# Opening of attention with other score banks, load order and transposes; next first operand ahead of the second matrix in units 1 to 4

## The chip, the cores and the metric

The kernel runs on one NeuronCore of one Trainium2 chip. The metric is the device time of one execution in microseconds (us). Engines are named as in the profile: PE (TensorE matmul), PEld (its weight loads), DVE (VectorE), ACT (ScalarE), POOL (GpSimd) and SP (SyncE, which only issues DMAs here). Each engine works through its own instructions in program order and waits on semaphores of the others.

## The reference, cut

Inputs: q, k, v of 4 batches, 8 heads, 576 positions, 64 wide; expert weights of 8 experts 512 to 1024 to 512; a last feed-forward of 512 to 2048 to 512 whose weights come as 64-bit floats.

```
scores = scale * q @ k.T                       # window of 128, causal, with a slope per head
attn   = softmax(where(mask, scores + bias, -1e9))
x      = (attn @ v) as 2304 tokens x 512
logits = x @ w_gate;  P = exp(logits - max);   8 rounds of row and column normalisation
x      = sum over 8 experts of P[:, e] * (relu(x @ w1[e]) @ w2[e])
h      = x @ w_in;  out = (h * cos(h)) @ w_out
```

## The kernel before

**Attention** (the first 156 us). Two heads make a pair; there are 16 pairs, and each has five groups of queries (u = 0 to 4), so 80 groups n. The loop takes two groups per turn i (n = 2i and 2i+1), and the program's order is that of the calls in it. A turn issues the scores of its groups on PE (`emit_qk`, L537 and L535), the exponentials of the turn before on ACT (`emit_exp`, L562), the maxima of its own groups on DVE (`emit_max`, L547), a step of the gate (`gates`), attention times v of turn i-4 (`emit_AV`, L639), the PE transposes of the next pair's q and k (`heads` and `emit_T`, L494; pieces 0 and 1 are q, 2 and 3 are k), the transposes of the probabilities of turn i-3 (`emit_PT`, L601 and L603), the normalisation on POOL (`emit_norm`, L586) and side work (`side`). A tile's name carries the pair or the group: T2_0 is piece 0 of pair 2, s6_0 a score bank of groups 6 and 7, pt0 the transposed probabilities of group 0.

**Banks.** PSUM has eight banks: two for scores (`ps_s`), three for transposes and probabilities (`ps_t`), two for `xbank` (where attention times v accumulates and pieces 1 and 3 of the transposes land), one for the gate and pieces 0 and 2 (`ps_g`). The scores of turns 1 and 3 are put into one half of `xbank` and one bank of `ps_t`, all others into `ps_s`. A piece in `xbank` waits for whoever still reads `xbank`.

**Loads.** All loads but the first k go through SP's queue, in program order. `load_heads` issues three DMAs for one operand of one pair into one of two buffers; q of pair p+2 is loaded behind the transposes of q of pair p+1. `load_raw` loads expert weights (two DMAs of 256 KB), `load_f64` a piece of the 64-bit weights into the buffer `u0`, and `convert_f64` turns one piece into 32-bit numbers in ten steps, one step per group, and loads the next piece in its eighth step.

**Gate.** `gates` first finishes an earlier half of 384 tokens (`gate_block2`: three small matmuls, a DVE copy L384) and then begins the next half (`gate_block`, L374), both in the one bank of `ps_g`.

**Experts.** The phase `moe, 0` has 32 units u; each takes seven products of 384 columns (L972, tiles x, y, z), and one `batch` of the unit before: six tiles of 128 tokens in `g2` (L1200 to L1202) into the banks gT0, gT1, gT2 in turn, each added to an accumulator by DVE (`evac`, L1181, later L1191). Beside it the next unit's operands are made in high and low halves: `prep_a` (first operand waX: three ACT copies L143, three DVE subtractions L146, a store L148), `prep_b` (second matrix wbX: ACT L160, POOL L162, three stores L167), `prep_s` and `prep_sb` (sums on POOL). They are generators in lists (`pre`, `sbq`), and `slot` takes a step of the first of each list between products and tiles. In `pre`, `prep_b` of a unit stands ahead of `prep_a` of the next. In units 0 to 3 eight rounds of `sinkhorn` (PE L420; DVE L410 to L412 and L421 to L423) run in the list `bg`.

Of the kernel before, what the change touches and what calls it, by code (L numbers as in the profile page):

```python
# [18 lines left out]
P = 128  # L19
# [10 lines left out]
def tile_attention_moe_cos_ffn(ctx, tc, q, k, v, w_gate, w1, w2, w_in, w_out, out):  # L30
# [42 lines left out]
    with tc.manual_schedule():  # L73
# [164 lines left out]
        f64_t = {}  # L238

        def load_f64(c):  # L240
            if c >= 4 * NU2:
                return
            s, x = divmod(c, 4)
            raw = u_pool.tile([P, 512, 2], I32, tag="u0", name=f"f64_{c}")
            if x < 2:
                for y in range(2):
                    kc = 2 * x + y
                    nc.sync.dma_start(
                        out=raw[:, y * FU:(y + 1) * FU, :].rearrange("p n t -> p (n t)"),
                        in_=w_in[kc * P:(kc + 1) * P, 2 * s * FU:2 * (s + 1) * FU],  # L250
                    )
            else:
                r0 = s * FU + (x - 2) * P
                nc.sync.dma_start(out=raw.rearrange("p n t -> p (n t)"), in_=w_out[r0:r0 + P, :])
            f64_t[c] = raw
# [266 lines left out]
        def emit_qk(n, pi, u):  # L522
            a = n % 2
            if n // 2 not in sbank:
                if n // 2 in (1, 3):
                    sbank[n // 2] = [xbank[:, :512], ps_t.tile([P, 512], F32, tag="t", name=f"s{n}_1")]
                else:
                    sbank[n // 2] = [ps_s.tile([P, 512], F32, tag="s", name=f"s{n}_{j}") for j in range(2)]
            grp[n] = sbank[n // 2] if a == 0 else sbank.pop(n // 2)
            c0, c1 = span(u)  # L530
            k0 = (u - 1) * P + c0
            for j in parts(u):
                o = grp[n][j][:, a * W2 + c0:a * W2 + c1]
                if u == NG - 1:
                    nc.tensor.matmul(o, qL[pi % 2], kT[pi][:, k0:k0 + c1 - c0])  # L535
                else:
                    nc.tensor.matmul(o, qT[pi % 2][hr[j], u * P:(u + 1) * P], kT[pi][hr[j], k0:k0 + c1 - c0])  # L537
# [126 lines left out]
        load_heads(0, k, kraw, "kr", nc.scalar, part=1)  # L664
        load_heads(1, q, qraw, "qr")
        load_heads(1, k, kraw, "kr")
        load_heads(0, v, vt, "v")
        make_identity(nc, ident)
        warm = ps_s.tile([P, 512], F32, tag="s", name="warm")

# [53 lines left out]
        distance(rel_li, rel_l, LW, hr)  # L724
        for t in qL:
            nc.gpsimd.memset(t, 0.0)
        load_heads(1, v, vt, "v")

        groups = [(pi, u) for pi in range(NP_ALL) for u in range(NG)]
        done_tok = 0  # L730
# [9 lines left out]
        def heads(n, pool=None):  # L740
            if n >= NGR:
                return
            pi, u = groups[n]
            if u < 4 and pi + 1 < NP_ALL:
                emit_T(pi + 1, u, pool)
                if u == 1:
                    load_heads(pi + 2, q, qraw, "qr")
                if u == 3:
                    load_heads(pi + 2, k, kraw, "kr")

        def side(n):
            nonlocal conv
            if n % 2 == 0 and n < 2 * NPAIR:
                set_last(n // 2)
            if n == 2:
                nc.sync.dma_start(out=wg_raw, in_=w_gate.rearrange("(k p) e -> p k e", p=P))
                nc.gpsimd.memset(wg, 0.0)
            if n == 3:
                load_f64(0)
            if 4 <= n < 8:  # L760
                load_raw((n - 4) // 2, "ab"[n % 2])
            if n == 8:
                nc.gpsimd.tensor_copy(wg[:, :, :E], wg_raw)
            if n == 12:
                conv += [prep_s(0), prep_a(0), prep_b(0), prep_s(1), prep_a(1), prep_b(1), prep_s(2)]
            if n == 48:
                early.append(stages(("moe", 0), xr[0]))
            if n == NGR:
                conv.append(prep_sb(0))
            if n == 56:  # L770
                early.append(combos(("moe", 0), xr[0]))
            if early and next(early[0], StopIteration) is StopIteration:
                early.pop(0)
            if 8 <= n < 50 and (chunk or n < 40):
                if not chunk:
                    chunk.append(convert_f64(n_f64[0]))
                    n_f64[0] += 1
                if next(chunk[0], StopIteration) is StopIteration:
                    chunk.pop(0)
            if n % 2 == 0 or 44 <= n < 56 or n >= 72:  # L780
                while conv and next(conv[0], StopIteration) is StopIteration:
                    conv.pop(0)

        def gates(n):
            nonlocal gate2, next_half
            for j, lT in gate2:
                gate_block2(j, lT, (ps_g, "g"))
            gate2 = []
            if n < NGR + 6 and next_half < 2 * NB and HB * (next_half + 1) <= done_tok:
                gate2.append((next_half, gate_block(next_half, (ps_g, "g"), ap_)))  # L790
                next_half += 1

# [3 lines left out]
        for i in range(NGR // 2 + 4):  # L796
            for g in pair(i):
                emit_qk(*g)
            for g in pair(i - 1):
                if g[0]:  # L800
                    emit_exp(*g)
            for g in pair(i):
                if g[0] != 1:
                    emit_max(*g)
            gates(2 * i - 2)
            if not i:
                emit_exp(*pair(0)[0])
                emit_T(0, 1, (ps_t, "t"))
                emit_T(0, 3, (ps_g, "g"))
                emit_max(*pair(0)[1])  # L810
            for g in pair(i - 4):
                emit_AV(*g)
            if i == 1:
                heads(0)
                heads(1)
                heads(2, (ps_t, "t"))
            elif i:
                if i == 2:
                    heads(3)
                heads(2 * i)  # L820
                heads(2 * i + 1)
            for n, pi, u in pair(i - 4):
                if u == NG - 1:
                    emit_x(pi)
                    load_heads(pi + 2, v, vt, "v")
                    if pi % NPAIR == NPAIR - 1:
                        done_tok += S
            for g in pair(i - 3):
                emit_PT(*g)
            if i < NGR // 2:  # L830
                emit_norm(pair(i - 1))
            else:
                for g in pair(i - 1):
                    emit_norm([g])
            for n in (2 * i, 2 * i + 1):
                side(n)
# [392 lines left out]
        def begin(n):  # L1229
            if n < len(steps):  # L1230
                kind, b, u = steps[n]
                if kind == "moe" and not b and u >= 2:
                    pre.append(prep_a(u))
            if n + 1 < len(steps):
                kind, b, u = steps[n + 1]
                if not b and kind == "moe" and u >= 3:
                    pre.append(prep_s(u))
# [168 lines left out]
```

## Time and profile before

| what | us |
|---|---|
| runs shown: median (lowest to highest of 3) | 1981.72 (1981.71 to 1982.1) |
| the profiled execution | 1982.96 |
| its span, first to last instruction | 1981.2 |
| attention, to the first expert product | 0 to 156.1 |
| expert phases and last feed-forward | 156.1 to 1981.2 |

The span is what all rows refer to; what lies around it is 1.76 us in the profiled execution. A row of a timeline gives start, duration, engine, line, operation, tiles and shape; in brackets stands the idle time of the engine just before it and what ended that. Matmul ends are modelled, so two neighbouring matmuls may overlap by a few tenths.

### The profile page before, as it was taken

Reading aid. Unit: us, or ns where it says so; the run is one execution under the profiler, and the core shown is the slowest. Engines: PE = TensorE matmul, PEld = TensorE weight load, DVE = VectorE, ACT = ScalarE, POOL = GpSimd, SP = SyncE. Lnnn points to the kernel's source line nnn. Section 1 sums busy time; section 2 is a strip of 40 time slices with the busy share of each in tenths; the row PEclk is TensorE's granted clock in tenths of the full one; section 3 lists DMA queues with packets and bytes.
Section 4 is the critical chain, followed back from the end, with each engine's and each line's share of the span. In section 5 each row is a group of like instructions: output and inputs, shape, how many; then the busy total and the mean of one; then the engine's idle time right before and its main releaser. Section 6 shows DMA issues by size and latency. Waiting matters only on the chain.

```text
span 1981.2 us, 31148 instructions
## 1 busy us (share of the span) xinstructions
PE 1957.6 (99%) x10977; PEld 1823.6 (92%) x10977; DVE 1555.7 (79%) x2655; ACT 862.6 (44%) x1617; POOL 964.7 (49%) x940
## 2 busy tenths in 40 slices
PE   8999999999999999999999999999999999999999
PEld 6668899999999999999999999999999999998898
DVE  7885777777777788988888877888877776757766
ACT  6885444444444333333333433333233354554543
POOL 5673566666666445454536622545454423333221
PEclk9999999999999999999999999999999999999999
DMA  7854888888888999998999888999998765554552
GB/s 194 221 141 146 294 294 312 302 310 311 295 309 302 321 333 314 339 336 320 340 326 326 277 285 280 328 337 334 330 306 297 242 223 195 197 218 175 207 192 96
DMA packets 293755, 540.05 MB, mean 273 GB/s; under 512 B 80256, under 2 KB 141792, under 8 KB 286432
## 3 DMA queue, kind: packets, MB, share of 16 engines
q1 hardware_dynamic: 292240, 537.74, 78.7%
q8 instruction: 87, 1.43, 0.3%
q14 instruction: 68, 0.56, 0.1%
q10 hardware_dynamic: 1360, 0.33, 0.1%
HBM read 384.32 MB, written 153.67 MB: 272 GB/s over the span
## 4 chain that ended last, share of the span: by engine, by line
PE 94%; DVE 2%; DMA 2%; ACT 1%; issue 1%; SPq 0%; POOL 0%; DVEq 0%; POOLq 0%; ACTq 0%
PE gT L1111 23%; PE y_moe L972 19%; PE z_moe L972 10%; PE gT L1201 7%; PE gT L1202 7%; PE gT L1200 7%; PE y_ffn L972 5%; PE x_moe L972 5%; PE z_ffn L972 2%; PE xbank L639 2%; DMA wbX<-wdp 1%; PE x_ffn L972 1%; PE s L537 1%; PE pt L603 1%; PE pt L601 1%
## 5 line engine op out<-in xcount | busy, mean ns | idle before, releaser
L1111 PE MATMUL gT<-hX,wbX 128*128 128x384 f32 x2688 | 538.7, 335 | 2.8 <-DMA wbX<-wdp 2.7
L1111 PEld LDWEIGHTS gT<-hX,wbX 128*128 128x128 f32 x2688 | 471.6, 188 | 5.5 <-DMA wbX<-wdp 2.1
L972 PE MATMUL y_moe<-xtT_moe,waX 128*128 128x384 f32 x1728 | 347.3, 335 | 0.0
L972 PEld LDWEIGHTS y_moe<-xtT_moe,waX 128*128 128x128 f32 x1728 | 304.4, 188 | 3.3 <-ACT s_moe L1001 0.6
L1123 DVE TENSOR_TENSOR acc_moe<-gT,acc_moe 128x384 f32<-128x384 f32 x432 | 237.7, 550 | 77.9 <-PE gT L1111 76.0
L1202 PE MATMUL gT<-wbX,hX 128*128 128x512 f32 x660 | 258.2, 391 | 0.0
L1201 PE MATMUL gT<-wbX,hX 128*128 128x512 f32 x660 | 258.1, 391 | 0.0
L1200 PE MATMUL gT<-wbX,hX 128*128 128x512 f32 x660 | 258.0, 391 | 0.0
L1001 ACT ACTIVATE s_moe<-y_moe 128x384 f32<-128x384 f32 x192 | 93.3, 486 | 350.5 <-PE y_moe L972 350.2
L1145 POOL TENSOR_TENSOR hodd<-hodd 128x384 f32<-128x384 f32 x128 | 156.0, 1238 | 139.2 <-DVE hX L1131 71.3
L1145 POOL TENSOR_TENSOR cX<-cX 128x384 f32<-128x384 f32 x128 | 145.7, 1158 | 157.3 <-DVE hX L1131 97.1
L961 POOL TENSOR_TENSOR hX<-cX,hX 128x768 fp32r<-128x768 f32 x44 | 83.5, 1913 | 249.3 <-ACT hX L958 208.6
L133 POOL TENSOR_TENSOR s<-ra 128x256 f32<-128x256 f32 x80 | 59.6, 745 | 236.5 <-DVE waX L146 164.0
L1191 DVE SCALAR_TENSOR_TENSOR acc_moe<-gT,prob,acc_moe 128x512 f32<-128x512 f32 x174 | 129.6, 747 | 37.5 <-PE gT L1202 35.7
L1202 PEld LDWEIGHTS gT<-wbX,hX 128*128 128x128 f32 x660 | 123.9, 188 | 25.9
L1200 PEld LDWEIGHTS gT<-wbX,hX 128*128 128x128 f32 x660 | 124.1, 188 | 25.5 <-DVE acc_moe L1191 0.7
L1201 PEld LDWEIGHTS gT<-wbX,hX 128*128 128x128 f32 x660 | 124.0, 188 | 24.3
L917 ACT ACTIVATE hX<-cX 128x768 fp32r<-128x768 f32 x64 | 43.9, 687 | 216.1 <-DVE cX L1004 216.1
L1131 DVE TENSOR_TENSOR hX<-cX,hX 128x768 fp32r<-128x768 f32 x112 | 131.4, 1173 | 1.6 <-ACT hX L1135 1.6
L1131 DVE TENSOR_TENSOR hX<-hodd,hX 128x768 fp32r<-128x768 f32 x112 | 127.4, 1137 | 0.9 <-ACT hX L1135 0.9
L972 PE MATMUL z_moe<-xtT_moe,waX 128*128 128x384 f32 x576 | 116.6, 336 | 2.6 <-DVE waX L146 2.6
L972 PE MATMUL z_moe<-xtB_moe,waX 128*128 128x384 f32 x576 | 116.1, 336 | 0.0
(211 smaller groups left out, 3768.3 us busy)
## 6 DMA issues: line engine op xcount, KB each, us to landing
waX<-wd SPq DMA_DIRECT2D x264, 512.0 KB, 5.5
wbX<-wdp SPq DMA_DIRECT2D x224, 512.0 KB, 6.6
wd<-waX SPq DMA_DIRECT2D x32, 1792.0 KB, 6.8
wdp<-sb SPq DMA_DIRECT2D x32, 1024.0 KB, 5.8
wdp<-wbX SPq DMA_DIRECT2D x96, 256.0 KB, 4.3
wbX<-wd SPq DMA_DIRECT2D x24, 1024.0 KB, 4.9
waX<-wd SPq DMA_DIRECT2D x88, 256.0 KB, 5.2
ra<-in_moe_w_dram SPq DMA_DIRECT2D x64, 256.0 KB, 7.3
```

The costliest lines, as they stand in the source:

```text
L133: nc.gpsimd.tensor_tensor(out=s4[:, o], in0=x, in1=y, op=op)
L961: eng.tensor_tensor(out=h[:, 1], in0=c, in1=h[:, 0].bitcast(F32), op=ALU.subtract)
L972: nc.tensor.matmul(ps[:, :HB], wa[:, WI[m], wl, kc, :], x[:, xl, kc, :], start=start and kc == 0 and n_ == 0, stop=stop and kc == 1 and n_ ...
L1001: nc.scalar.activation(out=t["s", i], in_=ps[:, :HB], func=AF.Copy)
L1111: nc.tensor.matmul(ps[:, :HB], w[:, u, wl, d * P:(d + 1) * P], x[:, xl, u, :], start=m in (1, 5, 2) and n_ == 0, stop=m in (4, 3, 2) and n ...
L1123: nc.vector.tensor_tensor(out=a, in0=ps[:, :HB], in1=a, op=ALU.add)
L1131: nc.vector.tensor_tensor(out=x[:, 1], in0=H[:, q], in1=x[:, 0].bitcast(F32), op=ALU.subtract)
L1145: nc.gpsimd.tensor_tensor(out=H[:, t[0], c], in0=H[:, t[1], c], in1=H[:, t[2], c], op=ALU.subtract)
L1191: nc.vector.scalar_tensor_tensor(out=a, in0=ps, scalar=pe, in1=a, op0=ALU.mult, op1=ALU.add)
L1200: nc.tensor.matmul(ps, hf[f][:, 0, ts], wb[:, f, 0, :], start=f == 0, stop=False)
L1201: nc.tensor.matmul(ps, hf[f][:, 0, ts], wb[:, f, 1, :], start=False, stop=False)
L1202: nc.tensor.matmul(ps, hf[f][:, 1, ts], wb[:, f, 0, :], start=False, stop=f == 1)
```

## The change

In attention: the scores of turn 1 go into two banks of `ps_t`, those of turn 3 into `ps_s`; in turn 3 the probabilities' transposes stand ahead of the heads' transposes; q and k are loaded one pair earlier (pair p+3 into the buffer that pair p+1 has just left); v of pairs 0 and 1 goes behind q of pair 2; the first three 64-bit pieces are loaded into the token buffer `xr[NB - 1]`, which is free until the last batches, at fixed groups (0, 12, 22, 32) and no longer behind a conversion; expert weights are loaded at groups 4, 18, 28, 38, not 4 to 7; conversions begin one group later; `gates` finishes a half or begins one, not both in a call. In the expert phase `prep_a` of units 2 to 5 is put at the head of `pre`.

```diff
         def load_f64(c):
-            if c >= 4 * NU2:
+            if c >= 4 * NU2 or c in f64_t:
                 return
             s, x = divmod(c, 4)
-            raw = u_pool.tile([P, 512, 2], I32, tag="u0", name=f"f64_{c}")
+            if c < 3:
+                spare = xr[NB - 1].rearrange("p k t -> p (k t)")[:, c * 1024:(c + 1) * 1024]
+                raw = spare.bitcast(I32).rearrange("p (n t) -> p n t", t=2)
+            else:
+                raw = u_pool.tile([P, 512, 2], I32, tag="u0", name=f"f64_{c}")
...
             if n // 2 not in sbank:
-                if n // 2 in (1, 3):
-                    sbank[n // 2] = [xbank[:, :512], ps_t.tile([P, 512], F32, tag="t", name=f"s{n}_1")]
-                else:
-                    sbank[n // 2] = [ps_s.tile([P, 512], F32, tag="s", name=f"s{n}_{j}") for j in range(2)]
+                pool, tag = (ps_t, "t") if n // 2 == 1 else (ps_s, "s")
+                sbank[n // 2] = [pool.tile([P, 512], F32, tag=tag, name=f"s{n}_{j}") for j in range(2)]
...
-        load_heads(0, v, vt, "v")
...
-        load_heads(1, v, vt, "v")
...
                 if u == 1:
-                    load_heads(pi + 2, q, qraw, "qr")
+                    load_heads(pi + 3, q, qraw, "qr")
                 if u == 3:
-                    load_heads(pi + 2, k, kraw, "kr")
+                    load_heads(pi + 3, k, kraw, "kr")
...
-            if n == 3:
-                load_f64(0)
-            if 4 <= n < 8:
-                load_raw((n - 4) // 2, "ab"[n % 2])
+            if n in (12, 22, 32):
+                load_f64(n // 10)
+            if n in (4, 18, 28, 38):
+                load_raw(n // 20, "ab"[n % 20 // 10])
...
-            if 8 <= n < 50 and (chunk or n < 40):
+            if 9 <= n < 50 and (chunk or n < 40):
...
-            for j, lT in gate2:
-                gate_block2(j, lT, (ps_g, "g"))
-            gate2 = []
-            if n < NGR + 6 and next_half < 2 * NB and HB * (next_half + 1) <= done_tok:
+            if gate2:
+                for j, lT in gate2:
+                    gate_block2(j, lT, (ps_g, "g"))
+                gate2 = []
+            elif n < NGR + 6 and next_half < 2 * NB and HB * (next_half + 1) <= done_tok:
...
                 emit_T(0, 3, (ps_g, "g"))
+                load_heads(2, q, qraw, "qr")
+                load_heads(0, v, vt, "v")
+                load_heads(2, k, kraw, "kr")
+                load_f64(0)
+                load_heads(1, v, vt, "v")
                 emit_max(*pair(0)[1])
+            if i == 3:
+                for g in pair(i - 3):
+                    emit_PT(*g)
...
-            for g in pair(i - 3):
-                emit_PT(*g)
+            if i > 3:
+                for g in pair(i - 3):
+                    emit_PT(*g)
...
                 if kind == "moe" and not b and u >= 2:
-                    pre.append(prep_a(u))
+                    pre.insert(0 if u <= UPE + 1 else len(pre), prep_a(u))
```

Line numbers in rows of the changed program are those of its own file (4 to 10 higher at the same statement).

PE in turn 3, before: the second q transpose of pair 2 (`xbank` from qr2) and the first k transpose T2_2 stand behind the scores s6 and ahead of the transposes of the probabilities pt0 and pt1.

```order
L537 MATMUL xbank_192<-kT1_379,qT1_189 128x256
L537 MATMUL s6_1_437<-kT1_379,qT1_189 128x256
L537 MATMUL xbank_192<-kT1_379,qT1_189 128x256
L537 MATMUL s6_1_437<-kT1_379,qT1_189 128x256
L494 MATMUL xbank_192<-ident_75,qr2_372 128x128 x3
L494 MATMUL T2_2_465<-ident_75,kr2_415 128x128 x2
L603 MATMUL pt0_470<-ident_75,sp_321 128x128
L603 MATMUL pt0_470<-ident_75,sp_323 128x128
L601 MATMUL pt0_470<-ident_75,sp_340 128x128
L603 MATMUL pt1_473<-ident_75,sp_340 128x128
L601 MATMUL pt0_470<-ident_75,sp_342 128x128
L603 MATMUL pt1_473<-ident_75,sp_342 128x128
```

PE in turn 3, changed:

```order
L539 MATMUL s6_0_442<-kT1_390,qT1_189 128x256
L539 MATMUL s6_1_443<-kT1_390,qT1_189 128x256
L539 MATMUL s6_0_442<-kT1_390,qT1_189 128x256
L539 MATMUL s6_1_443<-kT1_390,qT1_189 128x256
L605 MATMUL pt0_461<-ident_75,sp_313 128x128
L605 MATMUL pt0_461<-ident_75,sp_315 128x128
L603 MATMUL pt0_461<-ident_75,sp_350 128x128
L605 MATMUL pt1_464<-ident_75,sp_350 128x128
L603 MATMUL pt0_461<-ident_75,sp_352 128x128
L605 MATMUL pt1_464<-ident_75,sp_352 128x128
L498 MATMUL xbank_192<-ident_75,qr2_331 128x128 x3
L498 MATMUL T2_2_481<-ident_75,kr2_339 128x128 x2
```

Scores of groups 6 and 7 lie in s6_0 and s6_1 of `ps_s`, and the six transposes of the probabilities have moved ahead of the two pieces of pair 2.

SP behind the q and k loads of pair 1, before (qr2 and kr2 are q and k of pair 2, v0 and v1 the values of pairs 0 and 1, f64_0 the first 64-bit piece):

```order
L462 DMA v0_216<-in_v_dram 128x4x64 x2
L468 DMA v0_216<-in_v_dram 64x2x64
L462 DMA v1_309<-in_v_dram 128x4x64 x2
L468 DMA v1_309<-in_v_dram 64x2x64
L462 DMA qr2_372<-in_q_dram 128x4x64 x2
L468 DMA qr2_372<-in_q_dram 128x2x64
L756 DMA wg_raw_313<-in_moe_w_gate_dram 128x4x8
L248 DMA f64_0_391<-in_moe2_w_in_dram 128x512 x2
L462 DMA kr2_415<-in_k_dram 128x4x64 x2
L468 DMA kr2_415<-in_k_dram 128x2x64
```

SP at the same place, changed (xr2 is the token buffer that takes the 64-bit piece):

```order
L466 DMA qr2_331<-in_q_dram 128x4x64 x2
L472 DMA qr2_331<-in_q_dram 128x2x64
L466 DMA v0_335<-in_v_dram 128x4x64 x2
L472 DMA v0_335<-in_v_dram 64x2x64
L466 DMA kr2_339<-in_k_dram 128x4x64 x2
L472 DMA kr2_339<-in_k_dram 128x2x64
L252 DMA xr2_87<-in_moe2_w_in_dram 128x512 x2
L466 DMA v1_345<-in_v_dram 128x4x64 x2
L472 DMA v1_345<-in_v_dram 64x2x64
L466 DMA qr3_383<-in_q_dram 128x4x64 x2
```

q of pair 2 has moved ahead of both v, and k of pair 2 ahead of v1, the gate weights and the 64-bit piece.

DVE in the batch that stands in unit 3, which makes the low halves of unit 4's first operand (waX from ra4 and s4_4), before; gT0 to gT2 are the tiles of the batch, the rows on gT3 and prob are Sinkhorn's:

```order
L1181 TENSOR_TENSOR acc_moe0_2885<-gT2_2733,acc_moe0_2885 128x512
L1181 TENSOR_TENSOR acc_moe0_2885<-gT0_2731,acc_moe0_2885 128x512
L421 TENSOR_REDUCE gT3_2734<-gT3_2734 128x8
L422 RECIPROCAL gT3_2734<-gT3_2734 128x8
L423 SCALAR_TENSOR_TENSOR prob_81<-prob_81,gT3_2734 128x18x8
L146 TENSOR_TENSOR waX_88<-ra4_2914,waX_88 128x2x256
L1181 TENSOR_TENSOR acc_moe0_2885<-gT1_2732,acc_moe0_2885 128x512
L146 TENSOR_TENSOR waX_88<-ra4_2914,waX_88 128x256
L410 TENSOR_REDUCE gT3_2734<-prob_81 128x18
L411 RECIPROCAL gT3_2734<-gT3_2734 128x18
L412 TENSOR_TENSOR prob_81<-prob_81,gT3_2734 128x18x8
L146 TENSOR_TENSOR waX_88<-s4_4_3101,waX_88 128x4x256
```

DVE at the same place, changed:

```order
L146 TENSOR_TENSOR waX_88<-ra4_2913,waX_88 128x2x256
L1191 TENSOR_TENSOR acc_moe0_2884<-gT2_2732,acc_moe0_2884 128x512
L146 TENSOR_TENSOR waX_88<-ra4_2913,waX_88 128x256
L146 TENSOR_TENSOR waX_88<-s4_4_3100,waX_88 128x4x256
L1191 TENSOR_TENSOR acc_moe0_2884<-gT0_2730,acc_moe0_2884 128x512
L425 TENSOR_REDUCE gT3_2733<-gT3_2733 128x8
L426 RECIPROCAL gT3_2733<-gT3_2733 128x8
L427 SCALAR_TENSOR_TENSOR prob_81<-prob_81,gT3_2733 128x18x8
L1191 TENSOR_TENSOR acc_moe0_2884<-gT1_2731,acc_moe0_2884 128x512
L414 TENSOR_REDUCE gT3_2733<-prob_81 128x18
L415 RECIPROCAL gT3_2733<-gT3_2733 128x18
L416 TENSOR_TENSOR prob_81<-prob_81,gT3_2733 128x18x8
```

The three rows that write waX have moved up, ahead of the additions of the third and fourth tile; both triples of Sinkhorn and the fifth tile now stand behind them.

## Rows read from the trace of the kernel before

**Rows 1.** Page, part 1: busy time, share of span, instructions of TensorE.

```profile
PE 1957.6 (99%) x10977; PEld 1823.6 (92%) x10977; DVE 1555.7 (79%) x2655; ACT 862.6 (44%) x1617; POOL 964.7 (49%) x940
```

**Rows 2.** TensorE's waits, whole span: us in total, times, longest.

```profile
PE z_moe L972 <- DVE waX L146: 2.6, 3, 1.0
PE xbank L494 <- DVE anb L547: 2.2, 2, 1.3
...
PE T L494 <- DMA kr<-in_k_dram: 1.0, 1, 1.0
...
PE T L494 <- DMA qr<-in_q_dram: 0.7, 1, 0.7
```

**Rows 3.** Windows, all engines: stretch, length, busy times, granted clock, DMA share, GB/s.

```profile
10.00:19.00 9.00, 4.34 (x30) 2.93 (x31) 6.73 (x34) 3.98 (x16) 3.61 (x9) 1.00 0.84 210
19.00:23.00 4.00, 4.00 (x18) 2.18 (x16) 1.36 (x7) 2.56 (x9) 1.12 (x3) 0.57 1.10 316
24.00:60.00 36.00, 35.94 (x307) 24.75 (x306) 30.87 (x140) 33.51 (x110) 22.82 (x45) 1.00 0.73 181
```

**Rows 4.** Timeline of TensorE, opening of attention.

```profile
10.71 0.55 PE L494 MATMUL xbank<-ident,qr 128*128 128x128 f32 x3 [0.84 <-DVE anb L547]
...
14.36 0.41 PE L494 MATMUL T<-ident,qr 128*128 128x128 f32 x2 [0.65 <-DMA qr<-in_q_dram]
...
17.16 0.55 PE L494 MATMUL xbank<-ident,qr 128*128 128x128 f32 x3 [1.32 <-DVE anb L547]
18.75 0.41 PE L494 MATMUL T<-ident,kr 128*128 128x128 f32 x2 [1.04 <-DMA kr<-in_k_dram]
...
20.20 1.23 PE L537 MATMUL s<-kT,qT 64*128 64x256 f32 x4
...
22.30 0.79 PE L639 MATMUL xbank<-ptT,v 128*64 128x256 f32 x4
```

**Rows 5.** Timeline of VectorE, the same stretch.

```profile
11.29 0.48 DVE L502 TENSOR_SCALAR qT<-xbank,inv 128x256 f32<-128x256 f32 x1 [0.30 <-PE xbank L494]
...
13.73 0.28 DVE L547 CUSTOM_DVE_ANT_0 sp<-s,rel 128x128 f32<-128x128 f32 x1
...
15.98 0.42 DVE L547 CUSTOM_DVE_ANT_0 sp<-xbank,rel 128x256 f32<-128x256 f32 x1 [0.20 <-PE s L537]
```

**Rows 6.** Timeline of SP, its DMA issues, same stretch.

```profile
10.80 1.08 SPq L462 DMA_DIRECT2D qr<-in_q_dram  x2
...
14.06 0.93 SPq L462 DMA_DIRECT2D kr<-in_k_dram  x2
...
29.29 0.92 SPq L462 DMA_DIRECT2D v<-in_v_dram  x2
```

**Rows 7.** DMA issues of the first 30 us: count, size, median us to landing.

```profile
kr<-in_k_dram SPq DMA_DIRECT2D x8, 128.0 KB, 3.2
```

**Rows 8.** Timeline of TensorE, gate of the second batch.

```profile
94.69 0.85 PE L374 MATMUL gate<-xr,wg 128*32 128x384 f32 x8 [0.72 <-DVE logits L384]
...
100.91 0.44 PE L494 MATMUL T<-ident,kr 128*128 128x128 f32 x2 [0.64 <-DVE logits L384]
```

**Rows 9.** Timeline of TensorE, first products of expert units 4 and 5.

```profile
217.72 0.97 PE L972 MATMUL z_moe<-xtT_moe,waX 128*128 128x384 f32 x4 [1.00 <-DVE waX L146]
218.53 0.42 PE L420 MATMUL gT<-prob,ones 128*128 128x152 f32 x2
...
234.73 0.97 PE L972 MATMUL z_moe<-xtT_moe,waX 128*128 128x384 f32 x4 [0.64 <-DVE waX L146]
```

**Rows 10.** Timeline of VectorE, the ends of the batches in units 3 and 4.

```profile
216.45 1.22 DVE L146 TENSOR_TENSOR waX<-s,waX 128x1024 fp32r<-128x1024 f32 x1
...
230.22 1.41 DVE L1191 SCALAR_TENSOR_TENSOR acc_moe<-gT,prob,acc_moe 128x512 f32<-128x512 f32 x2
231.53 1.01 DVE L146 TENSOR_TENSOR waX<-ra,waX 128x512 fp32r<-128x512 f32 x1
```

**Rows 11.** Chain of work that ended last: first use of v of pair 2.

```profile
38.47 0.65 PE xbank L639 x4
```

## The prediction

> **What bounds the kernel now.** I read the page's busy shares first: TensorE is busy 99% of the span [rows 1], so time can be won only where it waits or runs slowly, and every instruction that leaves its path early moves all that follows. Then its waits [rows 2]: in three places of the first 240 us the edit touches what ended them: `xbank` pieces that waited for the maxima (2.2 us in two waits), transposes that waited for q and k of pair 2 (0.7 and 1.0), and first products of expert units that waited for the low half of waX (2.6 in three). The windows say what else the opening costs: from 10 to 19 us TensorE is busy 4.34 of 9 us, and behind that, from 19 to 23, the granted clock is 0.57 of full, near the lower of its two levels (1.2 against 2.4 GHz) [rows 3]. From 24 to 60 us it is busy 35.94 of 36 us, so that stretch is set by TensorE and an earlier start of it arrives whole, unless ScalarE, busy 33.51 us of it, or VectorE, 30.87, comes to set it [rows 3]. All behind 240 us keeps its order on TensorE, and I count no change there.
>
> **Part 1, the opening.** I follow TensorE's new order with the durations of today.
> - Today the second q piece of pair 1 starts at 10.71 after a wait of 0.84 for the last maximum of turn 1, because these scores lie in `xbank`; VectorE, which must copy the piece out, starts at 11.29 after idling 0.30 [rows 4, 5]. With the scores in `ps_t` the piece is there when VectorE ends the maxima, at about 10.92. Everything behind that copy comes 0.37 us earlier.
> - The first transpose of q of pair 2 waits 0.65 for its load, until 14.36 [rows 4]. Its load was issued at 10.80 behind two v loads [rows 6]; a v load takes 1.6 to 1.8 us of the queue (0.92 for its first two DMAs [rows 6] and its third, estimated from the same spacing). Ahead of both it is issued near 10.80 - 3.4 = 7.4 and no longer waited for: about 13.1 instead of 14.36.
> - Scores s6 would follow at once, but in `ps_s` they must now wait for the maxima of turn 2, which end today at 13.73 + 0.28 = 14.01 [rows 5], so near 13.65. **This is the added wait.** Queued behind s6 are the probabilities' transposes and both pieces of pair 2. I put s6 from 13.8 to 14.9, as long as today (from 14.70, behind the two transposes at 14.36 [rows 4], to some 0.2 ahead of its first maximum at 15.98 [rows 5]). Bounds of this edit by itself: nothing if the maxima are done when q of pair 2 is, 0.7 if not (13.1 to 13.8); the walk takes 0.7.
> - Today TensorE then waits 1.32 for the maxima before it may write the next piece to `xbank`, and 1.04 for k of pair 2, until 18.75 [rows 4]. In the new order six transposes fill the first of these waits, to 15.5 (0.11 each: three take 0.33, and the 0.55 of a row [rows 4] has a modelled tail of 0.22); then the pieces, free of the maxima, from 15.5 to 16.2. k of pair 2 is issued behind q of pair 2 and v of pair 0 only: 7.4 + 1.6 + 1.7 = 10.7, two DMAs to 11.7, and with the median landing of 3.2 us [rows 7] it is there at 14.9; with today's own (14.99 to 18.75, 3.8) at 15.5. Not waited for.
> - Scores s8 wait for the maxima of s6. VectorE starts them at 15.0, and four, 0.35 apart (0.42 with the overlap [rows 5]), end at 16.4. s8 runs from 16.5. Today s8 and the qL scores take 2.1 us, from 20.20 to 22.30 [rows 4], at half clock; at full clock 1.05. So attention times v of turn 4 starts at 17.55, not 22.30: **4.8 us**.
>
> Is the clock full there? From 10 to 16.5 TensorE now has about 2.1 us of idling, against 4.66 in the nine microseconds that come before the fall today [rows 3]; I take it that it stays up. If it falls all the same for as long as today (19 to 23 at 0.57), 0.43 x 4.0 = 1.7 us go back. The Trainium skill, "TensorE: Matmul & The Clock Gate", section "A second HAM failure mode: psum-queue depth-cycling", holds against the change: short idles between groups of matmuls that cycle PSUM banks were enough, in another kernel, to make the clock go down and up. By that rule the opening, which goes from banks in turn to one pair of banks, would keep its slow stretch, and the sum would be 5.5 instead of 7.2. The row shows the fall behind a stretch less than half busy, and no fall in the 36 us behind it [rows 3].
>
> Bounds of the part: below, 4.8 - 1.7 = 3.1; above, all idle and all loss of clock, 4.66 + 1.7 = 6.4.
>
> **Part 2, the gate.** In turn 25 the new half waits 0.72 for the logits of the old one, since both use the one bank of `ps_g`; in turn 26 the piece that follows waits 0.64 for the same copy [rows 8]. With one step per call, attention times v (about 1 us) stands between the finish and the piece in turn 25, which hides the copy: 0.7 saved. In turn 26 the piece now waits for ScalarE's copy of the gate, which stands behind four exponentials: I leave the 0.64 there. In the added turn 27 the finish again has attention times v behind it. **0.7 us**, bounds 0 and 1.4.
>
> **Part 3, units 3 to 5.** The first operand's three subtractions move up in VectorE's order; nothing is added, so what it had done at the end of a batch it has done at the same time. What changes is who is late.
> - Unit 4: the four matmuls that waited 1.00, until 217.72, may start at 216.72 and end 0.81 later at 217.53. The next on TensorE is Sinkhorn's matmul (218.53 today [rows 9]), and its prob is now *behind* the long subtraction of 1.14 us, which used to stand behind prob (1.22 from 216.45 [rows 10], overlapping the next by 0.08). So prob is ready at 217.6, and the matmul runs at 217.7: 0.8 won of 1.0. Unit 3 has the same rows: 0.8.
> - Unit 5, without Sinkhorn, waits 0.64 [rows 9]. There the first subtraction moves ahead of the addition that frees gT2 for the batch's last tile. The addition ends today near 230.9 (half of the pair from 230.22 [rows 10]); TensorE writes the bank at 231.0. Behind a subtraction as long as one addition (0.65, half of the pair's span) it ends at 231.5, behind one as long as today's 1.01 [rows 10] at 231.9: a **new wait of 0.5 to 0.9**. Net between +0.1 and -0.3; I take the +0.1.
>
> In all **1.7 us**; bounds -0.3 (if what is won at the first two is lost in the same bank) and 2.6 (the whole wait [rows 2]). Prep_b's POOL product and its three stores, pushed behind, are read a whole unit later (217.72 to 234.73, 17 us [rows 9]), and the store of waX goes out earlier; I cost both at nothing, and if POOL's product were late the next batch would wait for it, which needs some 6 us of delay.
>
> **Part 4, at nothing.** Expert weights and 64-bit pieces spread over 38 groups are used from group 9 on; fewer are in flight while q and k of pairs 2 and 3 land. Conversions one group later keep their count of instructions.
>
> **Sum:** 4.8 + 0.7 + 1.7 = 7.2 us. The profiled execution took 1982.96 us with a span of 1981.2; it would be 1975.8 with a span of 1974.0. It lies 1.24 above the median of the runs, 1981.72, so the median would be **1974.5**.
>
> **Rivals.**
> - *The clock falls anyway* (above): 1.7 back, 1976.2. For it: idles remain. Against: they are half as long.
> - *Given back in attention.* ScalarE is busy 93% of 24 to 60 us [rows 3]; it also caught up during today's stall, and without that pause it may set the pace, so that the 4.8 is gone by the first expert product. Left are 0.7 + 1.7: 1979.3. Against: in 36 us TensorE waited 0.06.
> - *The bank of the batch* eats all of part 3: 1976.2.
> - *The load isn't early enough.* If k of pair 2 takes 5 us from its second issue it lands at 16.7; s8 starts at 17.0 instead of 16.5: 1975.0. Inside the range, no case of its own.
> - *More is won*: other waits of attention, on maxima and ptT copies, shift too: all three parts near their upper ends, 6.4 + 1.4 + 2.1 = 9.9, give 1971.8.
> - *Slower: v behind waiting loads.* q and k of pair p+3 wait for transposes issued just before, and v of pair p+2 stands behind them in SP's queue. v of pair 2 is issued at 29.29 and used at 38.47 [rows 6, 11]: 9.2 us, less 1.0 for its issues and 3.2 for landing (k's median [rows 7]), 5.0 to spare. The transposes (0.8) and three issues (1.6) take 2.4 of it. Should landings grow by more than the 2.6 left, every v from pair 2 to 15 is late; to turn 7.2 won into 4 lost each would have to be late by 0.8, so landings of 6.6 us on average: 1985.7. The GB/s there is not full, and I give it little.
>
> **Chances.** Forecast 0.58, clock falls 0.11, bank 0.08, more won 0.09: all these are faster by over 0.2% (4 us, what a measurement of this kernel can tell from no change), 0.86. Given back: 0.10, within 0.2%. Slower 0.04. The range runs from 1971.8 to 1977.6: its lower end is that of more won, its upper end the clock fallen, nothing at the gate and some half of part 3 (3.1 + 0 + 1.0 = 4.1 won). It leaves out the given-back case, the slower one and half of more won.
>
> **What would show it.** Right: no `xbank` wait for maxima and no wait for kr in the first 20 us; attention times v of turn 4 at 17 to 18 us; clock 1.00 from 15 to 25; no gate wait for logits in turn 25; the first expert product about 5.5 us earlier than 156.1; z_moe waits of waX gone, with a short wait at Sinkhorn's matmul and one at gT2. Wrong: a clock near 0.5 there, new waits on ptT copies between 20 and 60 us, or long waits at tiles 5 and 6 of the batches of units 3 and 4.

## The result, and the profile after

The changed kernel took 1997.59 us (median of 6 runs, 1996.81 to 1999.77) beside 1983.11 for the kernel before (6 runs, 1981.71 to 1985.42): a ratio of 1.0075, 95% interval 1.0065 to 1.0086. I had forecast 1974.5 and faster; it is 14.5 us slower. The profiled execution took 1999.64 us with a span of 1997.8, against 1982.96 and 1981.2.

TensorE's busy time stands beside [rows 1]. It is longer by 5.5 us with the same 10977 matmuls (part of it ran at a lower clock), and the span has grown by 16.6, so some 11 us are idle time.

```profile
PE 1963.1 (98%) x10977; PEld 1827.8 (91%) x10977; DVE 1552.8 (78%) x2655; ACT 862.2 (43%) x1617; POOL 964.9 (48%) x940
```

TensorE's waits over the whole span stand beside [rows 2] (us in total, times, longest). The waits that the change aimed at (z_moe for waX, xbank for the maxima, transposes for q and k) are gone. The four long ones here are all new.

```profile
PE y_moe L982 <- ACT s_moe L1011: 7.6, 1, 7.6
...
PE gT L1210 <- DVE acc_moe L1201: 3.6, 1, 3.6
PE s L539 <- DVE anb L549: 2.8, 1, 2.8
PE gT L1210 <- DVE acc_moe L1191: 2.7, 2, 2.2
```

The windows say when. Columns: stretch, length, busy time of PE, PEld, DVE, ACT and POOL (with instructions), granted clock, DMA share, GB/s. The first row stands beside the first of [rows 3].

```profile
10.00:19.00 9.00, 7.38 (x54) 5.30 (x52) 8.53 (x47) 7.05 (x27) 4.73 (x12) 1.00 0.90 211
19.00:24.00 5.00, 5.00 (x48) 3.35 (x47) 3.87 (x19) 4.21 (x15) 2.59 (x7) 1.00 0.84 217
24.00:60.00 36.00, 34.89 (x290) 24.07 (x291) 29.97 (x131) 30.93 (x103) 21.71 (x40) 1.00 0.80 198
...
84.00:92.00 8.00, 8.00 (x49) 5.75 (x49) 6.21 (x25) 2.60 (x12) 4.18 (x7) 0.63 0.75 195
...
195.00:262.00 67.00, 52.24 (x239) 45.05 (x239) 39.62 (x76) 23.94 (x40) 28.35 (x30) 0.90 0.67 238
```

The opening did what was forecast: 7.38 us busy of 9 instead of 4.34, and the clock stays at 1.00. The loss is in two later places. The first is small, at 80 to 92 us. The second is the stretch of expert units 3 to 5, at 195 to 262, where TensorE is busy 52.24 of 67 us at a mean clock of 0.90; the same window before is this row:

```profile
195.00:262.00 67.00, 64.36 (x323) 57.30 (x322) 53.19 (x93) 31.22 (x51) 37.82 (x39) 1.00 0.85 298
```

**Reading the large loss.** The chain of waits through 196 to 262 us, of the changed kernel (start, length, what), is mostly a DMA: the store of sb, prep_sb's halves of the second operand. One turn of it:

```profile
218.93 0.33 SPq L148
...
219.36 0.39 SPq L105
...
219.80 0.95 SPq L105
...
220.80 9.84 DMA wdp<-sb
...
230.74 0.07 ACT sb L185
...
231.71 0.40 ACT waX L143
232.11 0.39 ACT s_moe L1011
232.52 0.57 DVE cX L1014
```

SP issues the 1792 KB store of waX (L148), two loads of ra (L105), and only then the store of sb, which lands 9.84 us later. SP takes its DMAs in program order, and at L148 it stands until VectorE has made the low halves of waX:

```profile
SPq L148 <- DVE waX L146: 39.7, 3, 16.6
```

The halves of sb were ready at 216.23 here (VectorE's L189 from 215.02, 1.21 long), 4.6 us before their store was issued at 220.80. ScalarE's next conversion writes the same single sb buffer, so it stands still until then, and the copy of s_moe that TensorE needs stands behind it. ScalarE's timeline shows the worst of the three turns, TensorE's shows what it costs:

```profile
253.73 1.06 ACT L185 ACTIVATE sb<-sb 128x1024 fp32r<-128x1024 f32 x1 [9.62 <-DMA wdp<-sb]
254.70 0.47 ACT L1011 ACTIVATE s_moe<-y_moe 128x384 f32<-128x384 f32 x1
```

```profile
213.68 0.50 PE L1210 MATMUL gT<-wbX,hX 128*128 128x512 f32 x1 [2.23 <-DVE acc_moe L1191]
...
235.40 0.50 PE L1210 MATMUL gT<-wbX,hX 128*128 128x512 f32 x1 [3.55 <-DVE acc_moe L1201]
255.22 2.29 PE L982 MATMUL y_moe<-xtT_moe,waX 128*128 128x384 f32 x6 [7.56 <-ACT s_moe L1011]
```

The waits named differ (acc_moe, s_moe), their root is one. In the kernel before SP's order was the other one. Its timeline of SP shows the store of sb ahead of the store of waX, in the same unit:

```profile
212.15 0.36 SPq L192 DMA_DIRECT2D wdp<-sb  x1
212.56 1.60 SPq L105 DMA_DIRECT2D rb<-in_moe_w_dram  x2
217.70 0.33 SPq L148 DMA_DIRECT2D wd<-waX  x1
218.07 1.43 SPq L105 DMA_DIRECT2D ra<-in_moe_w_dram  x2
```

The landing of the store (KB, median us; before, then changed) and ScalarE's two next conversions in the kernel before:

```profile
wdp<-sb SPq DMA_DIRECT2D x5, 1024.0 KB, 5.0
...
wdp<-sb SPq DMA_DIRECT2D x4, 1024.0 KB, 9.6
...
223.08 1.06 ACT L185 ACTIVATE sb<-sb 128x1024 fp32r<-128x1024 f32 x1 [1.14 <-POOL sb L182]
...
236.97 1.07 ACT L185 ACTIVATE sb<-sb 128x1024 fp32r<-128x1024 f32 x1 [0.23 <-POOL sb L182]
```

There it went out at 212.15 and, with the median landing of 5.0 us in that stretch, was done at 217.2; ScalarE's next conversion started at 223.08. The slack was 5.9 us. By the order of after it would leave at 217.70 + 0.33 + 1.43 = 219.5, 7.3 later, and land 4.6 slower (median 9.6). That is twice the slack. The turn behind it had less: the store of 230.36 was done at 235.4, 1.6 ahead of the conversion at 236.97, and this is the turn in which the changed kernel waits 9.62.

**Reading the small loss.** VectorE waits 4.25 us near 80 us. The chain through 70 to 86 us of the changed kernel:

```profile
77.33 0.47 SPq L105
...
77.83 1.35 SPq L105
...
79.24 0.02 SPq L294
...
79.28 3.72 DMA w<-fb
...
83.03 0.04 DVE fb L278
```

The store of a converted 64-bit piece (L294) is issued behind the raw loads of rb, at 79.28; VectorE wants that buffer for the next piece at 78.8 and stands until 83.03, the maxima behind it. In the kernel before the store went out at 75.67 and VectorE came at 82.50: the change has brought VectorE 3.7 us earlier and the store 3.6 us later. TensorE waits 2.79 for them, and from 84 to 92 its clock is 0.63 (0.50 in the first half).

### The profile page after: what moved, and what is told of

It reads as the page before. It is cut to its first block, busy times and chain, and to the rows that moved or that the text cites. A ratio compares the mean times of both kernels' runs of the same rounds, so it can differ in the third digit from the quotient of the medians.

```text
span 1997.8 us, 31149 instructions
## 1 busy us (share of the span) xinstructions
PE 1963.1 (98%) x10977; PEld 1827.8 (91%) x10977; DVE 1552.8 (78%) x2655; ACT 862.2 (43%) x1617; POOL 964.9 (48%) x940
## 3 DMA queue, kind: packets, MB, share of 16 engines
q8 instruction: 87, 1.43, 0.3%
## 4 chain that ended last, share of the span: by engine, by line
PE 92%; DMA 3%; DVE 2%; ACT 2%; issue 1%; POOL 0%; SPq 0%; ACTq 0%; POOLq 0%; DVEq 0%
PE gT L1121 23%; PE y_moe L982 19%; PE z_moe L982 10%; PE gT L1211 7%; PE gT L1210 7%; PE gT L1212 7%; PE y_ffn L982 5%; PE x_moe L982 5%; PE z_ffn L982 2%; PE xbank L641 2%; DMA wdp<-sb 2%; PE x_ffn L982 1%; PE s L539 1%; DMA wbX<-wdp 1%; PE pt L605 1%
```

## The experiments

Two theories for the large loss. **Queue**: SP's order alone. **Rivals**: the order on ScalarE and VectorE, or loads that attention hands over late. The small loss: **one buffer** that waits for a store, or a queue that is late as a whole. Each table row has its own runs of the kernel before beside it.

| kernel | us, median | before, same chip | ratio, 95% |
|---|---|---|---|
| units_only | 1997.56 | 1982.53 | 1.0058 to 1.0088 |
| units_back | 1982.50 | 1982.53 | 0.9987 to 1.0006 |
| sb_store_first | 1980.64 | 1982.53 | 0.9982 to 1.0001 |
| stores_swapped | 2003.85 | 1981.99 | 1.0092 to 1.0119 |
| ra_behind | 1991.78 | 1981.99 | 1.0037 to 1.0065 |
| fb_two | 1998.39 | 1982.53 | 1.0062 to 1.0092 |
| fb_third | 1993.47 | 1981.99 | 1.0041 to 1.0072 |
| both_mended | 1976.43 | 1981.99 | 0.9959 to 0.9982 |
| opening_only | 1983.96 | 1981.37 | 0.9998 to 1.0019 |
| spread_only | 1983.93 | 1981.37 | 1.0006 to 1.0024 |
| no_spread | 1981.53 | 1981.37 | 0.9986 to 1.0007 |

**units_only and units_back: which edit loses it.** One line, put alone into the kernel before, and taken alone out of the changed one:

```diff
-                    pre.append(prep_a(u))
+                    pre.insert(0 if u <= UPE + 1 else len(pre), prep_a(u))
```

> The kernel before with one edit alone: the next unit's first operand is prepared ahead of its second matrix in units 3 to 5. Queue theory: in SP's order the 1792 KB store of waX and two loads of ra now stand ahead of the store of sb; ScalarE's conversion of the next sb (one buffer) waits for that store, and TensorE waits for the copies of s_moe queued behind it. Then this edit alone loses what the changed kernel lost between its first expert product (157.32 against 156.06) and its end (16.6 us later): 16.6 - 1.3 = 15.3, so about 1998, with a wait of y_moe for s_moe of several us. Rival, the other edits: the units are late because attention hands over its loads and conversions in another order. Then this edit alone gives the 1.7 us forecast for it: about 1981.

> The changed kernel with that one edit undone (prep_a behind prep_b again in units 3 to 5). Queue theory: the units go as in the kernel before, and what is left is the first expert product 1.3 us later: 1983.1 + 1.3 = 1984.4. Rival, attention's other order of loads makes the units late: about 1997, with the waits for s_moe still there.

Measured: 15.0 us lost with the line alone, nothing lost without it (the 1.3 us expected to remain aren't seen). The waits of units_only are those of the changed kernel:

```profile
PE y_moe L972 <- ACT s_moe L1001: 7.7, 1, 7.7
...
PE gT L1200 <- DVE acc_moe L1191: 2.6, 1, 2.6
PE gT L1200 <- DVE acc_moe L1181: 2.5, 1, 2.5
```

So the whole large loss is that line's, and all other edits together give nothing that stands out of the noise. It doesn't yet say by which engine's order.

**sb_store_first: the line kept, SP's order put back.** Only the DMAs at the end of prep_a are held back until prep_sb has issued its own:

```diff
+            def store():
+                nc.sync.dma_start(out=wd1[u], in_=waX[:, u % 2].bitcast(F32))
+                if u + 2 < NU1:
+                    load_raw(u + 2, "a")
+            if 3 <= u <= UPE + 1:
+                held.append(store)
+            else:
+                store()
...
                 load_raw(u + 2, "b")
+            while held:
+                held.pop(0)()
```

> The changed kernel with prep_a ahead of prep_b as in it, but the store of waX and the loads of ra for units 3 to 5 are issued behind the store of sb and the loads of rb, as SP had them before. Queue theory: the conversion of sb finds its buffer free, no wait for s_moe; the first products that waited for waX before wait no more, so 1984.4 less up to 1.7: 1982.7 to 1984.4. Rival, the order on the engines: ScalarE and VectorE convert waX ahead of copies and evacuations, and that alone delays TensorE: above 1990, with waits for s_moe or acc_moe of several us.

Measured 1980.64, 1.9 below units_back and a little below the range expected. ScalarE waits for the store no more, and what is left of TensorE's waits between 195 and 262 us is short:

```profile
201.56 0.53 PE L431 MATMUL gT<-prob,ones 128*128 128x152 f32 x2 [0.31 <-DVE prob L423]
218.50 0.53 PE L431 MATMUL gT<-prob,ones 128*128 128x152 f32 x2 [0.31 <-DVE prob L423]
231.68 0.50 PE L1217 MATMUL gT<-wbX,hX 128*128 128x512 f32 x1 [0.47 <-DVE acc_moe L1208]
```

The rival that the order on ScalarE and VectorE is to blame falls: that order is unchanged here. The reordering on these two engines gives about what I had forecast for it (1.7), though 1.9 us is within the noise of the two runs: their intervals overlap.

**stores_swapped: SP's order alone, in the kernel before.** Prep_sb's store and loads of rb in units 2 to 4 are held until prep_a has issued its own; nothing else moves:

```diff
+            if 2 <= u <= UPE:
+                held.append(store)
+            else:
+                store()
...
                 load_raw(u + 2, "a")
+            while held:
+                held.pop(0)()
```

> The kernel before with nothing changed but SP's queue in units 2 to 4: the store of sb and the loads of rb are issued behind the store of waX and the loads of ra, instead of ahead. Queue theory: the store goes out at about 217.7 + 0.35 + 1.45 = 219.5 instead of 212.15 and lands some 9.5 us later, at 229, when ScalarE wants to write sb at 223.1: a wait of some 6 us in two or three units, with the copies of s_moe behind it: 1992 to 1998. Rival, the order on ScalarE and VectorE is needed for the loss: the store has slack, and the time stays at 1982.5 within 2.

Measured: 21.9 us lost, more than expected and more than the changed kernel lost. Here is ScalarE's wait in 195 to 262 us, where the kernel before has none on a DMA:

```profile
ACT sb L187 <- DMA wdp<-sb: 24.4, 3, 10.6
```

So SP's order is enough by itself: the store of sb behind the store of waX and the loads of ra. With sb_store_first it is also needed: the cause is shown from both sides. One difference that goes with the larger loss: VectorE makes the low halves of waX later here, so the halves of sb are ready at 217.91 and their store leaves at 225.38, 7.5 us behind them instead of 4.6.

**ra_behind: place and bytes.** In the changed kernel only the loads of ra move behind the store of sb; the store of waX stays ahead.

```diff
+            if 3 <= u <= UPE + 1:
+                held.append(u + 2)
+            elif u + 2 < NU1:
...
+            while held:
+                load_raw(held.pop(0), "a")
```

> The changed kernel with only the two loads of ra moved behind the store of sb in units 3 to 5; the 1792 KB store of waX stays ahead of it. If the place behind that store and its bytes make most of the delay: the store of sb goes out 1.4 us earlier and has 0.5 MB less ahead of it, some 2.7 us of each ScalarE wait (4.3, 4.7, 9.6), and 1990 to 1994 is left. Rival, the two loads make the delay: the waits for s_moe go and the time is 1981 to 1984.

Measured 1991.78, as expected. ScalarE's three waits add up to 12.1 us instead of 18.6, so the two loads make about a third of them, 2.2 us each time on average, and the place behind the store of waX the rest. Of that rest the wait for that store's data and its bytes are not told apart (the store of sb leaves 3.1 us behind its data, at 215.78, and lands in 9.2):

```profile
ACT sb L187 <- DMA wdp<-sb: 12.1, 3, 7.0
```

**fb_two and fb_third: the small loss.** One converted piece goes into the spare place that its raw data have left, so that the next needn't wait for a store:

```diff
+            if c == 2:
+                b = xr[NB - 1].rearrange("p k t -> p (k t)")[:, :512].bitcast(I32)
+            else:
+                b = u_pool.tile([P, 512], I32, tag="u2", name=f"fb{c}")
```

(fb_two has `c == 1`.)

> The changed kernel in which the second converted 64-bit piece goes to a place of its own, so that VectorE needn't wait for the store of the first. Buffer theory: the 4.2 us wait of VectorE at 79 us goes, with TensorE's 2.8 behind it and the lower clock that follows (0.63 from 84 to 92, 0.37 x 8 = 3.0): 5.8 less, 1997.6 - 5.8 = 1991.8. Rival, SP's queue is late as a whole there, so that TensorE waits for q, k or v next: 1 us or less, about 1997.

> The changed kernel in which the third converted 64-bit piece goes to a place of its own: the store that VectorE waits for at 79 us is the third one (38.54, 55.84 and 79.28 are the issues of the first three), so the kernel fb_two moved the wrong piece. Buffer theory: the wait of VectorE (4.2) and TensorE's behind it (2.8) go; with the clock that fell behind it (up to 3.0) that is 2.8 to 5.8: 1991.8 to 1994.8. Rival, SP's queue is late as a whole and q, k or v are waited for next: about 1997.

Fb_two gave nothing because I had miscounted: the store at 79 us is the third piece's, and VectorE still waits for it, 3.8 us. It says nothing on either theory. Fb_third has the wait gone, and the clock with it:

```profile
76.00:84.00 8.00, 8.00 (x78) 5.75 (x75) 6.84 (x31) 7.74 (x30) 5.62 (x11) 1.00 0.91 222
84.00:92.00 8.00, 8.00 (x61) 5.06 (x59) 5.67 (x31) 6.27 (x20) 6.88 (x14) 1.00 1.00 247
```

Its ratio is lower than the changed kernel's by 0.0018, 3.6 us of the 2.8 to 5.8 expected. The two intervals overlap, so the size is uncertain, but both_mended beside sb_store_first gives the same way, 0.0021 or 4.2 us. No wait for q, k or v takes its place: one buffer, then, not the queue as a whole.

**both_mended: the two mends together.**

> Both mends on the changed kernel: the store of sb ahead of that of waX, and the place of its own for the third converted piece. If the two losses are separate they add: 1980.6 less 2.8 to 5.8, so 1974.8 to 1977.8, about what the prediction gave for the change. Rival, the opening's gain is lost again at the next late transfer: 1980 or more.

Measured 1976.43 (6 runs, 1974.36 to 1978.14), ratio 0.997 with an interval below 1: 5.6 us faster than the kernel before, and the best version here. The first expert product starts at 152.65 (156.06 before), 3.4 of the 5.2 us by which its span is shorter, and from 195 to 262 us TensorE is busy 65.92 us at full clock, as in sb_store_first.

**opening_only, spread_only and no_spread: what the spread of the loads is worth.** Opening_only has of the change only the opening (banks, early q, k and v, transposes of turn 3). Spread_only has only the raw loads spread over the groups, the places for the 64-bit pieces and the conversions one group later. No_spread is sb_store_first without the spread. Their diffs are the pieces of the diff shown above.

> The kernel before with the opening alone: banks of turns 1 and 3, q and k three pairs ahead, the early loads of q, v and k, and the transposes of turn 3 ahead of the heads. Gate, units, raw loads and 64-bit pieces are as before. Meeting theory: the opening wins 5.1 us at the first product with v (22.30 to 17.18 in the changed kernel) and brings VectorE earlier to the 64-bit conversion, while the store it waits for is issued at 75.7 as before; it lands near 79.4 and VectorE wants it at about 82.5 - 4.5 = 78.0, a wait of 1.4 at most, half of it hidden: first expert product 3 to 4 us earlier than 156.06, and 1978 to 1980. Rival, the opening's gain is lost in attention by itself (ScalarE sets the pace): first product within 1 of 156.06, time 1981 to 1983.

> The kernel before with the spread alone: raw loads at groups 4, 18, 28 and 38, three 64-bit pieces in the last batch's place, conversions one group later. Meeting theory: the store goes out at about 79.3 behind the loads of k and rb and lands at 83.0, VectorE wants it at 82.5 + 2.2 (one group later): no wait, 1982 within 1.5. Rival, the spread by itself costs the 4.2 us wait: a wait of VectorE of some 4 us near 80, and 1985 to 1988.

> The changed kernel without the spread (raw loads and conversions as before) and with the store of sb ahead of that of waX: the opening, the gate and the units' part. If the opening meets no late transfer without the spread it equals the kernel with both mends, 1976.4 within 1.5; if the raw loads of the first groups cost the opening, or VectorE still waits for the store, 1978 or more.

By its median opening_only won nothing. Its profiled execution has attention times v of turn 4 at 17.23 like the changed kernel, but the first expert product at 154.49, only 1.6 us earlier than before. VectorE's timeline shows one place where the gain goes, a few us on:

```profile
22.01 0.43 DVE L263 TENSOR_SCALAR fa<-f 128x512 int32<-128x512 int32 x1 [2.99 <-DMA f<-in_moe_w_in_dram]
```

The first 64-bit piece, issued at 16.39, isn't there when the conversion wants it; TensorE waits 1.02 and 0.31 behind it, and from 24 to 28 us its clock is 0.69. In no_spread it waits there in the same way (1.04 and 0.31), this time with a clock of 1.00 from 24 to 28, and v itself is late as well (timeline of TensorE):

```profile
37.03 1.02 PE L644 MATMUL xbank<-ptT,v 128*64 128x256 f32 x4 [1.76 <-DMA v<-in_v_dram]
```

That profiled execution of opening_only took 1980.01, third fastest of eleven between 1979.48 and 1988.54, so it can't show what makes the median 1983.96; that stays open.

No_spread took 1981.53, the second of the two outcomes expected ("1978 or more"). Both_mended, at 1976.43, has the spread besides and no wait for the store either; its ratio is lower by 0.0027, 5.4 us, with intervals that don't meet. So with that wait gone the spread is worth some 5 us, and with the wait (sb_store_first, ratio 0.9991) nothing that stands out of the noise.

Spread_only loses about 2.6 us by the medians. VectorE's wait for the store is 1.0 us in it (at 88.31, the store issued at 84.19), none in opening_only (75.22, wanted at 80.88), 4.2 with both together. But its profiled execution took 1987.17, 3.2 above its median, and lost most at the opening, which is that of the kernel before: the clock is low until 28 us there (until 23 before), and the first expert product starts at 162.30.

```profile
10.00:19.00 9.00, 5.89 (x31) 3.40 (x29) 6.45 (x34) 4.73 (x20) 3.63 (x9) 0.74 0.83 207
19.00:24.00 5.00, 5.00 (x21) 3.24 (x20) 2.15 (x12) 2.56 (x9) 1.12 (x3) 0.50 1.01 221
...
24.00:28.00 4.00, 4.00 (x23) 3.14 (x19) 1.22 (x9) 2.18 (x6) 2.03 (x5) 0.50 0.43 97
```

So what the spread alone costs in the median isn't shown. I had expected opening_only at 1978 to 1980 and spread_only within 1.5 of 1982; the first is missed by 4 us, the second by 0.4.

## Why the prediction was wrong

**The step that failed** is in part 3: "the store of waX goes out earlier; I cost both at nothing". I had moved that DMA past others in SP's queue and asked only who reads its data. I didn't ask which DMA now stands behind it, nor what that one frees. It was the store of sb, and it frees a single buffer that ScalarE writes again 17.7 us after (205.38, then 223.08), the next time 13.9 (236.97). Worked out from the rows of before as above, 7.3 us later with 5.9 of slack, the step would have come out as a wait in each unit. I had looked at prep_b's product and its stores, and priced a delay for POOL ("some 6 us"); that this is near the slack of 5.9 is chance, it belongs to another product. The loss measured for this term is 15.0 us where I had 1.7 won.

**No rival of mine was this one.** The slower rival put the danger in SP's queue too, but at the loads of v in attention. With the spread that didn't happen; without it (no_spread) v was late by 1.76 once.

**The rest of part 3 was right.** With SP's order put back, z_moe's three waits for waX are gone [rows 2, 9]; Sinkhorn's matmul waits 0.31 twice (0.2 expected), gT 0.47 once (0.5 to 0.9 expected). Busy time in 195 to 262 us rises from 64.37 in units_back to 65.92 in sb_store_first: 1.55 won, 1.7 forecast.

**Part 1 was right in size and wrong in one row.** Attention times v of turn 4 starts at 17.18 (17.55 forecast, 22.30 before [rows 4]): 5.1 us, where I had 4.8. It varies from execution to execution: 17.18 to 17.86 in the profiles with the new opening, 22.17 to 23.57 in those with the old one. The forecast wait of s6 for the maxima doesn't occur. Instead TensorE waits 1.62 for an exponential at 12.22, where it had waited 0.9 for a sum of VectorE's before (arr, L579):

```profile
12.22 0.49 PE L539 MATMUL s<-kT,qT 64*128 64x128 f32 x4 [1.62 <-ACT sp L564]
```

The clock stayed at 1.00 from 10 to 24 us, against 0.57 from 19 to 23 before [rows 3]; the rival in which it falls anyway is out. In the four profiles with the old opening (before, units_only, stores_swapped, spread_only) the clock is at 0.58 or less from 19 to 22 us, in those with the new one it is 1.00 there. The rule of the Trainium skill that I had weighed ("TensorE: Matmul & The Clock Gate", section "A second HAM failure mode: psum-queue depth-cycling") doesn't show in the changed kernel: its opening cycles one pair of banks with short idles and no fall up to 76 us.

**Part 4, "at nothing", was wrong in both directions.** The spread takes the load of the first 64-bit piece and v off the opening's way (3.0 us of VectorE in both kernels that have the opening without it, 1.76 of TensorE in no_spread), and together with the opening it costs the wait at 80 us. The gain is seen only with the wait mended (no_spread beside both_mended). Both hang on where a store or load stands in SP's queue.

**"Given back in attention"** came true, with another cause than the one I named. I had looked at ScalarE's pace; it was VectorE behind a store. From turn 4's product to the first expert product the kernel before takes 156.06 - 22.30 = 133.8 us, the changed one 157.32 - 17.18 = 140.1. Of the 6.4 more, 2.8 are the wait and 0.37 x 8 = 3.0 the lower clock behind it. So the first expert product is 1.3 later where I had it 5.5 earlier. The last 0.6 I can't put to one row: new waits for an exponential (0.69 at 33.89) and for ScalarE's conversion of wbX (0.8) stand against a shorter one at the gate. Fb_third, without the wait, takes 152.44 - 17.23 = 135.2 over the same stretch, so by these profiles 4.9 of the 6.4 hang on the wait, not quite the 5.8 of the rows.

**Part 2** gave 0.6 (busy time in 92 to 130 us: 34.80 before, 35.36 after), forecast 0.7: the wait of 0.72 is gone, that of 0.64 [rows 8] is 0.79.

Put together: 14.5 slower is the 15.0 of SP's order and an opening whose 5.1 is given back within attention. With both mended the kernel took 5.6 us less than before, against the 7.2 of the sum.

## What to carry to other kernels

When work is moved, list for each DMA that it issues what stands behind it in the same queue, and for each of those which buffer its completion frees and when that buffer is written next; a store is waited for by its buffer's next writer long before anyone reads the data. Compare the new issue time plus the landing behind the larger transfer with that moment. An early gain can bring an engine sooner to a buffer whose store leaves no sooner (here 3.7 us earlier and 3.6 later), so slack that was counted at the old pace must be counted again at the new one.

## What the runs showed of the hardware

Behind the 1792 KB store and two loads of 256 KB the 1024 KB store of sb took 9.6 us to land (median), with the loads alone moved away 9.2, and 5.0 in its old place. The page "DMA: Bandwidth & Descriptors" of the Trainium skill, section "Issuing engines are not separate DMA queues", says that issuing from several engines saves only the time to initiate a DMA. No run here issued the store of sb from another engine, so whether that would have spared SP's part of the delay wasn't tried.

The clock fell behind short idles as well: in the changed kernel TensorE's idle of 2.79 us up to 83.99 was followed by 0.50 of full from 84 to 88 us, and the idle of 3.55 up to 235.40 by 0.59 from 236 to 240. In fb_third, without the first idle, the clock is 1.00 in both windows from 76 to 92. Not every short idle was followed by a fall: behind the 2.23 us up to 213.68 it is 1.00 from 212 to 220. By these rows the clock behind the idle of 2.79 cost about as much again, 0.37 x 8 = 3.0 us; the kernels without that idle gained 3.6 and 4.2 us by their ratios, less than the two together.

```profile
84.00:88.00 4.00, 4.00 (x22) 2.85 (x24) 3.78 (x16) 1.08 (x6) 2.79 (x5) 0.50 1.07 283
...
236.00:240.00 4.00, 4.00 (x12) 3.01 (x11) 4.00 (x7) 2.74 (x6) 1.78 (x2) 0.59 0.00 0
```
